# Six plain chunk pairs instead of eight in a fused attention and MLP kernel, with the last v, the exponential, the x additions and three steps of the group schedule moved

## The chip, the core and the metric

The kernel runs on one core of one Trainium2 chip. The metric is the device time of one execution in microseconds: the median of 3 runs before is 1306.22 us (1305.91 to 1307.12). In the text PE is TensorE (matmuls), PEld its weight loads, DVE is VectorE, ACT ScalarE, POOL GpSimd and SP SyncE; an engine executes its instructions in their order. POOL and SP here mostly issue DMAs.

## The reference

Tokens S = 2048, width D = 576, hidden F = 4608. All numbers are float32.

```python
xn = layernorm(x)
return x + A(xn) + B(xn)
# A: q, k, v = heads of xn @ wqkv (32 heads of 18); each token looks at itself and
#    7 earlier tokens, 2 apart; softmax of q.k * 18**-0.5; weighted sum of v; @ wo
# B: h  = gelu(layernorm(xn) @ w1), its four quarters shifted by +1, -1, +2, -2 tokens
#    x1 = xn + h @ w2
#    return x1 + gelu(layernorm(x1) @ w3) @ w4
```

## The kernel before

To keep float32 accuracy on PE, each operand is split into a high part and a low part (a copy on ACT, a subtraction on DVE), and a product is the sum of high x high, high x low and low x high. D = 576 is four and a half times 128, so such a product over D is 14 matmuls of 128 x 512.

The stages follow one another: the norms and q, k, v (written to DRAM as qkvd), the mixing with w1 and w2, then the large MLP (w3, w4) with the attention woven in as background work, and last the product with wo.

**The MLP.** F is cut into 36 chunks of 128, taken in 18 pairs. The first NPL = 8 pairs (line 37) are *plain*: for each pair and each of four blocks of 512 tokens there is a *unit* (loop at line 960) with two `up` (28 matmuls of 512 columns, then gelu) and four `down` of the unit before (48 matmuls of 288 columns). The other NWP = 10 pairs go through *groups* (loop at line 1130): a group treats one pair and 1024 tokens by a Strassen-Winograd scheme in seven products of seven matmuls (49 of 512 columns) and eight downs (96 of 288). There are NQ = 2 x NWP groups; the first NWP take tokens 0 to 1023, the rest tokens 1024 to 2047. In group NWP - 1 and the start of group NWP the seven operands of the second half are read again from DRAM (`get_op`, line 875) and split (`split_op`, line 885). In the code z is the unit's or the group's number counted from the end: z = -1 is the last.

**The order inside a group** is written out by hand: `ORDER` (line 1125) lists products P1 to P7 and downs D0 to D7 as "P1 P2 D0 P6 D1 P5 D2 P7 D3 P4 D4 P3 D5 D6 D7", and `at(item, f)` hangs further work on an item: loads of w3 and w4 (`load_pair`, line 905; `load_w4`, line 554), splits (`split_a`, `split_s`, `split_w4`, line 562), `combine` (line 916), which makes the sums and differences of w3 blocks in place, gelus and their low parts. `keep` (line 1070) copies a product from PSUM on ACT, `z_add` (line 1073) adds a product to it on DVE. A down's result goes either to Y in SBUF (DVE, line 841) or, for the ten token tiles in YD, through a staging tile (ACT, line 836) and an accumulating DMA on POOL's queue to DRAM (line 837). In PSUM two banks alternate for the downs.

w3's raw tile (`w3st`) has one buffer: `load_pair` fills it, `split_a` reads the parts A11, A22 and A12, one of its steps through an accumulating DMA (line 929), `combine` overwrites it, `split_s` reads it with another such DMA, and only then may the next load start.

**The attention** (line 677) is a generator over eight groups of four heads. For each it multiplies q with eight shifted views of k (L735) and sums (L738), adds the mask, takes the maximum and subtracts it, issues the exponential on ACT (L753), and then runs `av` (line 699) for the four heads before: weights times v (L711) summed into po (L715), and a store of po to DRAM (`od`, line 717). q, k, v and po have one buffer each. The load of the next v (line 759) is issued after that store. `bg(us, late)` (line 763) pulls pieces of the generator until a debt of microseconds is used up; each piece yields its assumed cost in us. A piece that yields None holds the generator until a call with `late`: in the plain units every second down, in the groups the item P6. In units 4 and on the rate is 9.4 us for each unit (none in the last two), in the groups 1.6 us for each item less what the group's own DVE work is assumed to cost. At group z = -6, item P4, the attention must be done; its SBUF room then goes to `o_turn` and `load_o` (lines 1108 to 1123), which turn od's tiles (DVE transposes, lines 160 and 161) in groups z = -5 to -2, and `put_o` writes them back for the wo product.

**The other steps that the change touches.** `sums` (line 858) builds the operands T1 to T4 in DRAM in units 5 to 19, by accumulating DMAs on POOL's queue. `load_xa` and `add_x` (lines 845 and 853) add x again: for tiles in YD by an accumulating DMA on POOL's queue, for the six others by a load on SP's queue into one buffer and an addition on DVE one unit later. In the last group w4's last pair is loaded (line 1144) ahead of wo, and split at D2 (line 1228).

Of the kernel before, what the change touches and what calls it, by code (L numbers as in the profile page):

```python
# [10 lines left out]
AF = mybir.ActivationFunctionType  # L11
# [22 lines left out]
YD = (1, 2, 3, 5, 7, 9, 10, 11, 13, 15)  # L34


NPL = 8
NWP = NF // 2 - NPL


# [17 lines left out]
def fused_block(ctx, tc, x, wqkv, wo, w1, w2, w3, w4, out):  # L58
# [618 lines left out]
    def attention(ap):  # L677
        mask = ap.tile([128, TPP, W], F32, name="mask")
        pool.memset(mask, 0.0)
        for w in range(1, W):  # L680
            pool.memset(mask[0:1, 0:DIL * w, W - 1 - w:W - w], -1e9)
        mask4 = mask[:, :, None, :].to_broadcast([128, TPP, GH, W])
        halo = HALO
        qs, ks, vs, Ls, den = {}, {}, {}, {}, {}
        po = ap.tile([128, 2, TPP * GC], F32, name="po")
        o = po[:, 0, :].rearrange("p (x d) -> p x d", d=HD)
        prod = po[:, 1, :].rearrange("p (x d) -> p x d", d=HD)

        def load(name, sel, g, lead, sp=sp):
            t = ap.tile([128, TPP + (halo if lead else 0), GC], F32, name=name)  # L690
            r = sel * NG + g
            sp.dma_start(t[:, (halo if lead else 0):, :],
                         qkvd[r, halo:, :].rearrange("(p j) d -> p j d", p=128))
            if lead:
                sp.dma_start(t[:, :halo, :],
                             qkvd[r, 0:S, :].rearrange("(p j) d -> p j d", p=128)[:, 0:halo, :])
            return t

        def av(g):
            L, v = Ls[g], vs[g]  # L700
            Lf = L.rearrange("p j h w -> p (j h) w")
            dve.tensor_reduce(den[g], Lf, axis=AX.X, op=ALU.add)
            dve.reciprocal(den[g], den[g])
            yield 0.8
            dve.tensor_tensor(Lf, Lf, den[g][:, :, None].to_broadcast([128, TPP * GH, W]),
                              op=ALU.mult)
            yield 0.6
            for w in range(W):
                vv = v[:, DIL * w:DIL * w + TPP, :].rearrange("p j (h d) -> p (j h) d", d=HD)
                dst = prod if w else o  # L710
                dve.tensor_tensor(dst, vv, Lf[:, :, w:w + 1].to_broadcast([128, TPP * GH, HD]),  # L711
                                  op=ALU.mult)
                yield 1.35
                if w:
                    dve.tensor_tensor(o, o, dst, op=ALU.add)  # L715
                    yield 1.35
            sp.dma_start(od.rearrange("(p j) d -> p j d", p=128)[:, :, g * GC:(g + 1) * GC],
                         po[:, 0, :].rearrange("p (j c) -> p j c", c=GC))

        yield None  # L720
        qs[0], ks[0] = load("q", 0, 0, False, pool), load("k", 1, 0, True, pool)
        vs[0] = load("v", 2, 0, True, pool)
        yield None
        for g in range(NG + 1):
            if g < NG:
                q, k = qs[g], ks[g]
                L = Ls[g] = ap.tile([128, TPP, GH, W], F32, name="L", bufs=2)
                Lf = L.rearrange("p j h w -> p (j h) w")
                Lw = Lf.rearrange("p x w -> p w x")
                qf = q.rearrange("p j d -> p (j d)")  # L730
                for w, n in ((0, 1), (1, 1), (2, 2), (4, 2), (6, 2)):
                    dst = po[:, 2 - n:2, :]
                    win = bass.AP(tensor=k.tensor, offset=k.offset + DIL * w * GC,
                                  ap=[list(k.ap[0]), [DIL * GC, n], [1, TPP * GC]])
                    dve.tensor_tensor(dst, qf[:, None, :].to_broadcast([128, n, TPP * GC]), win,  # L735
                                      op=ALU.mult)
                    yield 0.15 + 1.2 * n
                    dve.tensor_reduce(Lw[:, w:w + n, :],  # L738
                                      dst.rearrange("p w (x d) -> p w x d", d=HD),
                                      axis=AX.X, op=ALU.add)  # L740
                    yield 0.15 + 1.2 * n
                if g + 1 < NG:
                    qs[g + 1], ks[g + 1] = load("q", 0, g + 1, False), load("k", 1, g + 1, True)
                mx = den[g] = ap.tile([128, TPP * GH], F32, name="mx", bufs=2)
                dve.tensor_tensor(L, L, mask4, op=ALU.add)
                yield 0.6
                dve.tensor_reduce(mx, Lf, axis=AX.X, op=ALU.max)
                yield 0.6
                dve.tensor_tensor(Lf, Lf, mx[:, :, None].to_broadcast([128, TPP * GH, W]),
                                  op=ALU.subtract)  # L750
                yield 0.6
                yield None
                act.activation(L, L, AF.Exp, scale=float(HD) ** -0.5)  # L753
                if g == 0:
                    yield 4.0
            if g:
                yield from av(g - 1)
                if g < NG:
                    vs[g] = load("v", 2, g, True)

    state = {"gen": None, "debt": 0.0, "hold": False, "done": False}

    def bg(us, late=True):
        if state["gen"] is None or state["done"]:
            return
        state["debt"] = min(state["debt"] + us, 4.0)
        while state["debt"] > 0 and (late or not state["hold"]):
            cost = next(state["gen"], False)
            if cost is False:
                state["done"] = True  # L770
                return
            state["hold"] = cost is None
            state["debt"] -= cost or 0.0


    def temp(t, n=512):
# [183 lines left out]
    for u, (c, b) in enumerate(units):  # L960
# [79 lines left out]
            load_w4(NPL)  # L1040
        if 5 <= u < 21 and u % 2:
            sums((u - 5) // 8, (u - 5) % 8 // 2)
        if 13 <= u < 13 + NT:
            load_xa(u - 13)
        if 14 <= u < 14 + NT:
            add_x(u - 14)
    close_ab()


# [80 lines left out]
    for q in range(NQ):  # L1130
# [6 lines left out]
        if z == -1:  # L1137
            evc_pool.__exit__(None, None, None)
            opc.__exit__(None, None, None)
            EV[0] = (9, 11, 10, 2)  # L1140
            wop = tc.tile_pool(name="wop", bufs=1, reuse_waits="tile")
            wopool = wop.__enter__()
            Wo = wopool.tile([128, 10, D], F32R, name="Wo")
            load_w4(p)
            for k in range(5):
                load_wo(k)
        if q == NWP:
# [64 lines left out]
        elif z < -1:  # L1212
            at("P1", load_w4, p)
            at("D1", split_a, n, (0, 1))
            at("D2", split_a, n, (2,))
            at("P7", combine, n)
            at("D3", split_w4, p, 0)
            at("P4", gelu22)
            at("P4", split_w4, p, 1)
# [5 lines left out]
            if z < -2:  # L1225
                at("D6", load_pair, q + 2 + (q == NWP - 2))
        else:
            at("D2", split_w4, p)
            at("D3", gelu22)
            at("D4", low22)  # L1230
            at("D5", gelu12)
            at("D6", low12)
# [9 lines left out]
        if -4 <= z < -1:  # L1242
            at("P1", put_o, z + 4)
        if z == -2:
            at("D7", put_o, 3)

        if z == -1:
# [134 lines left out]
```

## Time and profile before

| | |
|---|---|
| median of 3 runs | 1306.22 us |
| lowest and highest run | 1305.91 and 1307.12 us |
| the profiled execution | 1301.97 us |
| its span, first to last instruction | 1300.2 us |
| mean granted clock of PE | 0.993 |
| HBM traffic, read and written | 119.73 and 107.28 MB |

Everything but the first three rows of this table is taken from the one profiled execution; the runs beside it carry no profile. "Busy" is the time in which an engine executes; PE's weight loads overlap its matmuls and are counted apart. In rows of waits the engine and the line that waited stand on the left, what it waited for on the right. In rows of time the columns are the start, the length, the engine with its line, the operation, output and inputs, and in brackets the idle time ahead of it with what ended it. SPq and PEq are the engines' sequencers, which issue DMAs and wait.

### The profile page before, as it was taken

Reading aid. Unit: us, or ns where it says so; the run is one execution under the profiler, and the core shown is the slowest. Engines: PE = TensorE matmul, PEld = TensorE weight load, DVE = VectorE, ACT = ScalarE, POOL = GpSimd, SP = SyncE. Lnnn points to the kernel's source line nnn. Section 1 sums busy time; section 2 is a strip of 40 time slices with the busy share of each in tenths; the row PEclk is TensorE's granted clock in tenths of the full one; section 3 lists DMA queues with packets and bytes.
Section 4 is the critical chain, followed back from the end, with each engine's and each line's share of the span. In section 5 each row is a group of like instructions: output and inputs, shape, how many; then the busy total and the mean of one; then the engine's idle time right before and its main releaser. Section 6 shows DMA issues by size and latency. Waiting matters only on the chain.

```text
span 1300.2 us, 19681 instructions
## 1 busy us (share of the span) xinstructions
PE 1266.0 (97%) x7538; PEld 1161.7 (89%) x7538; DVE 944.6 (73%) x1261; ACT 598.2 (46%) x952; POOL 245.2 (19%) x358
## 2 busy tenths in 40 slices
PE   8999999999999999999999999999959999999999
PEld 8999998899888998989899889999848999988898
DVE  6456535778469999999999889999859654665442
ACT  3322226526534434344346656556546555554530
POOL 2011100021221212222221222222112222222100
PEclk9999999999999999999999999999979999999999
DMA  7646874256887878988788777776796658899972
GB/s 210 156 111 143 172 166 144 71 147 177 203 247 152 174 170 202 233 145 223 146 205 185 136 171 159 154 161 112 161 228 106 129 110 180 174 209 195 255 242 83
DMA packets 201374, 219.16 MB, mean 169 GB/s; under 512 B 79152, under 2 KB 137744, under 8 KB 201152
## 3 DMA queue, kind: packets, MB, share of 16 engines
q1 hardware_dynamic: 168912, 151.57, 41.0%
q0 software_dynamic: 32368, 66.34, 31.9%
q8 instruction: 59, 0.97, 0.3%
q14 instruction: 35, 0.29, 0.1%
HBM read 119.73 MB, written 107.28 MB: 175 GB/s over the span
## 4 chain that ended last, share of the span: by engine, by line
PE 78%; DMA 10%; DVE 4%; issue 4%; ACT 2%; SPq 1%; POOL 0%; DVEq 0%; POOLq 0%; ACTq 0%
PE ps L832 27%; PE ps L214 16%; PE cc L1065 13%; PE p L813 13%; PE ps L466 4%; PE ps L313 3%; DMA w3st<-in_B_w_dram 2%; DMA x1n<-xn 1%; DMA yd<-Y 1%; DMA xn<-st 1%; DMA xt<-xn 1%; DMA w3a<-w3st 1%; DMA xt<-xd 1%; DMA wr<-in_A_wo_dram 1%; PE ps L481 1%
## 5 line engine op out<-in xcount | busy, mean ns | idle before, releaser
L832 PEld LDWEIGHTS ps<-w,c 128*128 128x128 f32 x3456 | 474.5, 188 | 27.5 <-DVE Y L841 8.8
L832 PE MATMUL ps<-w,c 128*128 128x288 f32 x3456 | 486.1, 295 | 10.8 <-DVE Y L841 7.0
L837 POOL DMA_DIRECT2D yd<-Y x154 | 137.0, 894 | 464.7 <-ACT Y L836 388.4
L836 ACT COPY Y<-ps 128x576 f32<-128x576 f32 x154 | 97.9, 636 | 151.4 <-PE ps L832 96.5
L807 DVE TENSOR_TENSOR c<-Y,c 128x512 fp32r<-128x512 f32 x144 | 98.4, 685 | 58.8 <-ACT Y L796 42.3
L214 PE MATMUL ps<-WQ,xt 128*128 128x432 f32 x672 | 134.8, 360 | 0.0
L214 PEld LDWEIGHTS ps<-WQ,xt 128*128 128x128 f32 x672 | 125.6, 188 | 5.7
L1065 PE MATMUL cc<-xt,w3s 128*128 128x512 f32 x420 | 108.3, 398 | 13.5 <-DVE Y L1075 13.5
L841 DVE TENSOR_TENSOR Y<-ps,Y 128x576 f32<-128x576 f32 x108 | 81.2, 751 | 49.2 <-PE ps L832 49.0
L1065 PEld LDWEIGHTS cc<-xt,w3s 128*128 128x128 f32 x420 | 76.7, 190 | 27.6 <-DVE Y L1075 14.0
L711 DVE TENSOR_TENSOR po<-v,L 128x1152 f32<-128x1152 f32 x64 | 86.1, 1353 | 14.7 <-DMA v<-qkvd 13.8
L735 DVE TENSOR_TENSOR po<-q,k 128x2304 f32<-128x2304 f32 (+1 forms) x40 | 82.9, 2073 | 13.9 <-issue 11.6
L795 ACT ACTIVATE c<-p 128x512 fp32r<-128x512 f32 x64 | 38.2, 597 | 115.8 <-PE p L813 115.8
L738 DVE TENSOR_REDUCE L<-po 128x128 f32<-128x2304 f32 (+1 forms) x40 | 82.8, 2069 | 0.4
L1071 ACT COPY Y<-cc 128x512 f32<-128x512 f32 x60 | 35.1, 584 | 97.4 <-PE cc L1065 94.1
L121 POOL TENSOR_TENSOR rs<-rs,mhalf 128x1 f32<-128x1 f32 x48 | 30.9, 643 | 258.8 <-DVE rs L120 148.0
L715 DVE TENSOR_TENSOR po<-po 128x1152 f32<-128x1152 f32 x56 | 75.8, 1353 | 0.8
L323 ACT COPY stg<-ps 128x864 f32<-128x864 f32 x24 | 21.2, 881 | 102.8 <-PE ps L214 60.5
L1065 PE MATMUL cc<-x1n,w3a 128*128 128x512 f32 (+1 forms) x280 | 67.9, 393 | 0.0
L1065 PEld LDWEIGHTS cc<-x1n,w3a 128*128 128x128 f32 (+1 forms) x280 | 51.6, 188 | 10.3
L214 PE MATMUL ps<-W,h 128*128 128x288 f32 x384 | 53.5, 295 | 0.0
L813 PE MATMUL p<-xt,w3s 128*128 128x512 f32 x224 | 52.4, 390 | 0.0
(188 smaller groups left out, 1892.6 us busy)
## 6 DMA issues: line engine op xcount, KB each, us to landing
yd<-Y POOLq DMA_DIRECT2D x156, 288.0 KB, 5.2
Y<-in_B_w_dram SPq DMA_DIRECT2D x27, 576.0 KB, 6.7
w3st<-in_B_w_dram SPq DMA_DIRECT2D x52, 256.0 KB, 6.3
qkvd<-stg SPq DMA_DIRECT2D x24, 432.0 KB, 3.5
yd<-ev POOLq DMA_DIRECT2D x26, 288.0 KB, 6.4
xd<-st SPq DMA_DIRECT2D x16, 320.0 KB, 6.0
xd<-big SPq DMA_DIRECT2D x16, 320.0 KB, 7.4
w3st<-in_B_w_dram SPq DMA_DIRECT2D x76, 64.0 KB, 6.5
```

Source lines behind the costliest of these rows:

```text
L214: pe.matmul(ps[:, h, :n], xs(a), ws(b, h), start=i == 0, stop=i == len(PAIRS) - 1)
L711: dve.tensor_tensor(dst, vv, Lf[:, :, w:w + 1].to_broadcast([128, TPP * GH, HD]), op=ALU.mult)
L715: dve.tensor_tensor(o, o, dst, op=ALU.add)
L735: dve.tensor_tensor(dst, qf[:, None, :].to_broadcast([128, n, TPP * GC]), win, op=ALU.mult)
L738: dve.tensor_reduce(Lw[:, w:w + n, :], dst.rearrange("p w (x d) -> p w x d", d=HD), axis=AX.X, op=ALU.add)
L807: dve.tensor_tensor(h[:, 1, :], g, h[:, 0, :].bitcast(F32), op=ALU.subtract)
L813: pe.matmul(ps, W3[f][:, w, :], x1n[b][:, a, :], start=n == 0, stop=n == len(PAIRS) - 1)
L832: pe.matmul(ps[:, k, :HF], h[:, col], w[:, p, k * HF:(k + 1) * HF], start=n == 0, stop=n == len(seq) - 1)
L836: act.copy(e.rearrange("p (h c) -> p h c", h=2), ps[:, :, :HF])
L837: pool.dma_start(yd[t], e, accum_op=ALU.add)
L841: dve.tensor_tensor(yv, ps[:, :, :HF], yv, op=ALU.add)
L1065: pe.matmul(ps, WX[w][:k, v, SLOT[w], :], area[sb][xk][:k, a, :], start=onto is None and i == 0, stop=last and i == len(HALVES) - 1, skip_ ...
```

## The change

The number of plain pairs falls from 8 to 6, so 24 units stand ahead of 24 groups of 12 pairs. The loads and additions of x start with unit 6 instead of 13. In the attention the exponential is put aside (`state["exp"]`) and issued by the next call of `bg` with `late`, by the next exponential, or ahead of the last `av`; the generator does not hold. The last four heads' v is loaded into k's buffer, as soon as the last scores are formed and their maximum is subtracted. `combine` moves from item P7 to D3 in the ordinary groups. The last pair's w4 is loaded at D7 of group z = -2, ahead of `put_o(3)`, instead of at the start of the last group; in the last group `split_w4` goes from D2 to D3 and `gelu22` from D3 to P4.

```diff
-NPL = 8
+NPL = 6
 NWP = NF // 2 - NPL
...
         def av(g):
+            if g == NG - 1:
+                exp_now()
             L, v = Ls[g], vs[g]
...
                 yield 0.6
-                yield None
-                act.activation(L, L, AF.Exp, scale=float(HD) ** -0.5)
+                exp_now()
+                state["exp"] = lambda L=L: act.activation(L, L, AF.Exp, scale=float(HD) ** -0.5)
+                if g == NG - 1:
+                    vs[g] = load("k", 2, g, True)
                 if g == 0:
                     yield 4.0
             if g:
                 yield from av(g - 1)
-                if g < NG:
+                if g < NG - 1:
                     vs[g] = load("v", 2, g, True)
 
-    state = {"gen": None, "debt": 0.0, "hold": False, "done": False}
+    state = {"gen": None, "debt": 0.0, "exp": None, "done": False}
+
+    def exp_now():
+        if state["exp"]:
+            state["exp"]()
+            state["exp"] = None
 
     def bg(us, late=True):
         if state["gen"] is None or state["done"]:
             return
+        if late:
+            exp_now()
         state["debt"] = min(state["debt"] + us, 4.0)
-        while state["debt"] > 0 and (late or not state["hold"]):
+        while state["debt"] > 0:
             cost = next(state["gen"], False)
             if cost is False:
                 state["done"] = True
                 return
-            state["hold"] = cost is None
-            state["debt"] -= cost or 0.0
+            state["debt"] -= cost
...
-        if 13 <= u < 13 + NT:
-            load_xa(u - 13)
-        if 14 <= u < 14 + NT:
-            add_x(u - 14)
+        if 6 <= u < 6 + NT:
+            load_xa(u - 6)
+        if 7 <= u < 7 + NT:
+            add_x(u - 7)
...
             Wo = wopool.tile([128, 10, D], F32R, name="Wo")
-            load_w4(p)
...
-            at("P7", combine, n)
+            at("D3", combine, n)
             at("D3", split_w4, p, 0)
...
         else:
-            at("D2", split_w4, p)
-            at("D3", gelu22)
+            at("D3", split_w4, p)
+            at("P4", gelu22)
...
         if z == -2:
+            at("D7", load_w4, NPL + pair(q + 1))
             at("D7", put_o, 3)
```

## The prediction

> **What bounds the kernel now.** I read the page first, then the busy time by stretches, then PE's waits, then the order of time around each place where PE stood.
>
> ```profile
> PE 1266.0 (97%) x7538; PEld 1161.7 (89%) x7538; DVE 944.6 (73%) x1261; ACT 598.2 (46%) x952; POOL 245.2 (19%) x358
> ```
>
> PE is the bound as a whole: it is busy 1266.0 of 1300.2 us, so time goes away only with matmuls or with one of PE's few gaps.
>
> ```profile
> 500.00:709.00 209.00, 208.57 (x1243) 189.89 (x1243) 199.96 (x187) 87.47 (x138) 49.54 (x57) 1.00 0.86 183
> ...
> 766.00:927.00 161.00, 161.00 (x967) 146.30 (x966) 152.90 (x168) 94.14 (x145) 38.22 (x45) 1.00 0.72 148
> 927.00:977.00 50.00, 35.17 (x209) 31.49 (x208) 31.70 (x36) 25.29 (x39) 7.76 (x9) 0.86 0.89 208
> 977.00:1138.00 161.00, 161.00 (x961) 146.18 (x961) 101.78 (x140) 91.90 (x146) 38.26 (x45) 1.00 0.70 140
> ```
>
> The columns are stretch, length, then busy us of PE, PEld, DVE, ACT, POOL, the granted clock, DMA share and GB/s. Plain units (500 to 709) and groups with attention on DVE (766 to 927) leave PE without a gap although DVE is 95% busy; groups without attention (977 to 1138, from 1011 on) bring DVE down to 63%. The exception is 927 to 977 with the clock at 0.86, where the first half of the tokens gives way to the second.
>
> ```profile
> DVE po L711 <- DMA v<-qkvd: 13.8, 1, 13.8
> PE cc L1065 <- DVE Y L1075: 13.5, 1, 13.5
> ```
>
> Totals, times, longest. DVE stood once for the last heads' v; PE stood behind it, because the z_add that frees a PSUM bank (L1075) was queued behind the waiting L711.
>
> **The change, part by part.**
>
> *Two plain chunks become four groups.* Starts of successive ups (28 matmuls) and of successive P1 (14):
>
> ```profile
> 502.35 6.38 PE p L813 x28
> ...
> 693.25 6.39 PE p L813 x28
> ...
> 788.00 3.23 PE cc L1065 x14
> ...
> 908.57 3.23 PE cc L1065 x14
> ```
>
> Fifteen units take 693.25 - 502.35 = 190.90 us, 12.73 each. Five groups with attention take 120.57 us, 24.11 each. A group does the work of two units, so it saves 2 x 12.73 - 24.11 = 1.35, and four save 5.4 us. The price is attention: eighteen units (4 to 21) carry it instead of twenty-six, and in the built order it now ends early in group 18 instead of group 11.
>
> ```profile
> L711 DVE TENSOR_TENSOR po<-v,L 128x1152 f32<-128x1152 f32 x64 | 86.1, 1353 | 14.7 <-DMA v<-qkvd 13.8
> ...
> L735 DVE TENSOR_TENSOR po<-q,k 128x2304 f32<-128x2304 f32 (+1 forms) x40 | 82.9, 2073 | 13.9 <-issue 11.6 <-DMA od<-po 1.8
> ```
>
> The groups that it fills hold eight or nine operations of 1.35 us, or five or six of 2.07, some 11 us each, as groups 1 to 8 held before. So DVE stays at the 95% that the stretch 766 to 927 stood. Value 5.4; ends 2 (each newly filled group loses a few tenths) and 6.4.
>
> *The last v goes into k's buffer.* SP's queue around the wait:
>
> ```profile
> 941.51 1.74 SPq L883 DMA_DIRECT2D x1n<-xn  x3
> 945.87 0.53 SPq L717 DMA_DIRECT2D od<-po  x1
> 946.45 2.22 SPq L692 DMA_DIRECT2D v<-qkvd  x1
> ```
>
> v has one buffer, so its load is issued only when the previous heads are finished, behind their store of po; for the earlier heads the next scores come between, for the last nothing. In the changed order the last v is loaded right after the last scores, before the previous heads' weighted sum (fifteen operations of 1.35 us), so that wait goes. What is late next?
>
> ```profile
> 945.83 1.06 ACT L892 ACTIVATE x1n<-x1n 128x1024 fp32r<-128x1024 f32 x1 [4.51 <-DMA x1n<-xn]
> ...
> 947.59 0.63 ACT L894 ACTIVATE x1n<-x1n 64x512 fp32r<-64x512 f32 x1
> 962.37 0.64 ACT L836 COPY Y<-ps 128x576 f32<-128x576 f32 x1 [14.15 <-PE ps L832]
> ```
> ```profile
> 957.45 3.29 PE L1065 MATMUL cc<-xt,w3s 128*128 128x512 f32 x7 [13.54 <-DVE Y L1075]
> ...
> 977.09 3.39 PE L1065 MATMUL cc<-x1n,w3a 128*128 128x512 f32 x14
> ```
>
> Without the wait P3 starts at 957.45 - 13.54 = 943.9 and, at some 1.6 us each, it and the down after it end near 947.1, before ACT is through with its first operand (947.59 + 0.63 = 948.2). Of ACT's 50.00 - 25.29 = 24.7 idle us in 927 to 977 these two waits are 18.7: behind them its split_ops stand nearly unbroken, so ACT bounds the rest of the stretch, and all of it moves up by ACT's 14.15 us. One thing may not follow: the second operand's load was issued until 941.51 + 1.74 = 943.25.
>
> ```profile
> 936.26 9.55 DMA x1n<-xn
> ```
>
> Landing like the first one (9.55 us after its first issue; the second's began near 940.4) it is there at 949.9, and ACT wants it at 948.8: 1.1 lost. Value 14.15 - 1.1 = 13.0; ends 6 (the first rival) and 15.
>
> *The x additions.* They move from units 13 to 29 to units 6 to 22.
>
> ```profile
> L855 DVE TENSOR_TENSOR Y<-Y,rz 128x576 f32<-128x576 f32 x6 | 4.5, 750 | 0.0
> ```
>
> Six of 0.75 us on DVE, ten accumulating DMAs on POOL's queue and six loads on SP's, none more than before. In 500 to 709 they lay beside units that ran without a gap; in units 6 to 13 they meet the T sums on the same POOL queue. If the cover were gone, they cost 4.5. Value 0.5; ends 0 and 4.5.
>
> *The exponential put aside* changes no instruction; the generator goes on instead of holding until P6. Four exponentials fall into groups instead of two.
>
> ```profile
> L753 ACT ACT_TABLE_LOAD x8 | 10.3, 1283 | 0.1
> ...
> 795.08 1.28 ACT L753 ACT_TABLE_LOAD   x1
> ```
>
> Each brings two table loads of 1.28 us. The one at 795.08 lies in the five groups above, which cost 24.11: hidden, 0; if ACT were late, two more groups lose up to 2 x 1.28 + 0.63 = 3.2 each.
> The Trainium skill, "ScalarE: Activation LUTs", section "What ACT_TABLE_LOAD costs", adds 1380 ns of drain to each load, which speaks against this part: an estimate from it, four more switches unhidden, is 5.5 us more, 1287. No wait of PE in this trace shows such a cost.
>
> *combine goes from P7 to D3.* In most groups the order on DVE stays as it was. In the four groups that turn the attention's result, P7's o_turn now comes ahead of combine:
>
> ```profile
> 1132.53 0.68 DVE L807 TENSOR_TENSOR c<-Y,c 128x512 fp32r<-128x512 f32 x1
> 1135.61 2.34 DVE L921 TENSOR_TENSOR w3st<-w3st 128x384 f32<-128x384 f32 x4 [2.40 <-issue]
> 1137.87 0.70 DVE L160 STREAM_TRANSPOSE big<-Y 128x512 f32<-128x512 f32 x1
> 1138.50 0.27 DVE L161 STREAM_TRANSPOSE big<-Y 128x128 f32<-128x128 f32 x1
> ```
> ```profile
> 1140.73 3.44 PE L832 MATMUL ps<-w,c 128*128 128x288 f32 x24 [1.45 <-DVE Y L841]
> ...
> 1166.02 3.44 PE L832 MATMUL ps<-w,c 128*128 128x288 f32 x24 [0.95 <-DVE Y L841]
> ...
> 1191.81 3.44 PE L832 MATMUL ps<-w,c 128*128 128x288 f32 x24 [1.47 <-DVE Y L841]
> ```
>
> DVE stands 2.40 us ahead of combine and then turns for 0.9 (1137.87 to 1138.77) while PE waits for the down's addition behind it. The turn fits into the idle time, and the addition comes 0.9 earlier: 3 x 0.9 = 2.7. Ends 0 (the turn's input late) and 3.9 (all three waits).
>
> *The last w4 is loaded one group earlier*, ahead of put_o, and split at D3.
>
> ```profile
> 1202.21 1.94 SPq L559 DMA_DIRECT2D Y<-in_B_w_dram  x1
> ```
> ```profile
> 1210.73 1.15 ACT L566 CAST w<-Y 128x1152 fp32r<-128x1152 f32 x1 [5.58 <-DMA Y<-in_B_w_dram]
> ```
> ```profile
> 1212.42 2.79 PE L1065 MATMUL cc<-xt,w3a 128*128 128x512 f32 x7 [2.72 <-ACT Y L1071]
> 1215.01 2.43 PE L832 MATMUL ps<-w,c 128*128 128x288 f32 x12
> 1217.28 1.78 PE L1065 MATMUL cc<-xt,w3s 128*128 128x512 f32 x7
> ```
> ```profile
> 1214.00:1216.00 2.00, 2.00 (x8) 1.71 (x8) 0.47 (x1) 1.17 (x2) 0.16 (x1) 0.50 1.05 249
> ```
>
> The load is issued at 1202.21, ACT waits 5.58 for it, and the copy that PE's P4 needs stands behind. Its raw place is free once the previous split is done, just ahead of the addition that PE awaits at 1191.81, so the load starts some 10 us earlier; the wait goes. PE gains 2.72 and the slow clock after it: 7 matmuls in 2.79 instead of 1.78 and 12 in 2.43 instead of the 1.75 of a usual down, 1.7 more. Value 4.4; ends 2 (the reads of wo and o late next) and 5.
> The Trainium skill, "TensorE: Matmul & The Clock Gate", section "What's actually happening", lets the clock fall only after an idle window of about 3.4 us; by that this gap would cost 2.72 alone and the sum be 1283.2. The trace differs: clock 0.50 after a 2.72 us gap.
>
> **The sum.** 5.4 + 13.0 - 0.5 + 2.7 + 4.4 = 25.0 us. Against the profiled execution's 1301.97 us (span 1300.2) that gives 1277.0. The runs' median is 1306.22, 4.25 longer than the profiled one; I take the gain from the median: 1281.2.
>
> **The rivals.**
> 1. *The middle is bound by the operands' loads.*
>
> ```profile
> 940.00:945.00 5.00, 3.92 (x23) 3.14 (x21) 0.36 (x1) 0.59 (x1) 0.00 (x0) 1.00 1.06 318
> ```
>
> The DMA engines are full there. If each of the five later operands comes 1.4 us after ACT wants it, 7 of the 13.0 are lost: 1288. Against it: the store and the v load leave this place in the queue.
> 2. *The x additions cost their full 4.5* in the fuller units: 1285.2.
> 3. *DVE waits at the same place for something else*, for instance the store of po that the next scores overwrite, now issued after all operand loads. It would have to last as long as v did; the 13.0 are lost: 1294. Against it: two scores that use the other half, and the splits, lie between.
> 4. *Slower: filled groups miss the w3 loop.* Load, split, combine and the next load form a ring; where it didn't close in time, P1 came 25.78 us apart:
>
> ```profile
> 1118.40:1144.18 25.78, 24.33 (x146) 21.97 (x146) 14.65 (x25) 13.37 (x21) 5.62 (x8) 1.00 0.95 213
> ```
>
> If attention delays combine so in all eighteen groups that carry it, 18 x 1.67 = 30 us eat the gain: 1311. It decides where DVE demand passes a group's 24.1 us, at some 12 us of attention in every group; for it speaks DVE's 95%, against it the 24.11 of five such groups.
>
> **How the numbers follow.** Forecast 0.76 (its own span 1275 to 1286), first rival 0.11, second 0.05, third 0.04, slower 0.04. The range 1275 to 1290 takes in the first three, and leaves out the last two and a little of the forecast's edges. 0.2% is 2.6 us, about what a measurement tells from no change: faster 0.95, within 0.01, slower 0.04.
>
> **What would show it.** Right: no wait of DVE for v; PE's wait of 13.5 gone and the clock at 1.00 through the middle; P1 near 24.1 apart in groups with attention after the middle too; waits for L841 in the late groups under 0.6; no wait of ACT for w4. Wrong: a new wait of DVE for a DMA, ACT waiting for operand loads at each split, units 6 to 13 over 12.73, or groups near 25.7.

## The result, and the profile after

The changed kernel takes 1296.15 us (median of 6 runs, 1294.97 to 1301.92) beside 1305.39 for the kernel before: a ratio of 0.9936, 95% interval 0.9917 to 0.9956. It is faster, by 9.2 us where 25.0 were forecast, and outside the range of 1275 to 1290. The profiled execution took 1294.97 us with a span of 1293.2, 7.0 less than before.

Busy time of the engines, from the page after; then stretches of its time with the columns of the prediction's table (groups 1 to 10, the middle, groups 12 to 17, groups 18 and 19, the three late groups):

```profile
PE 1263.3 (98%) x7510; PEld 1159.4 (90%) x7510; DVE 966.4 (75%) x1295; ACT 617.2 (48%) x978; POOL 252.5 (20%) x366
```
```profile
634.65:887.12 252.47, 243.88 (x1452) 220.67 (x1451) 226.41 (x251) 144.85 (x222) 59.63 (x70) 0.99 0.70 150
887.12:920.50 33.38, 29.36 (x171) 26.64 (x170) 27.48 (x30) 21.32 (x33) 6.06 (x7) 0.95 1.04 257
920.50:1065.60 145.10, 141.92 (x848) 128.41 (x847) 133.16 (x152) 85.90 (x134) 34.31 (x41) 1.00 0.65 133
1065.60:1113.72 48.12, 48.12 (x292) 43.88 (x291) 31.57 (x45) 26.53 (x42) 11.95 (x15) 1.00 0.80 170
1113.72:1191.31 77.59, 74.50 (x438) 67.43 (x437) 45.10 (x75) 40.24 (x63) 17.70 (x21) 0.98 0.92 214
```

The middle went from 44.62 to 33.38 us, near the forecast. But the groups that carry attention, which had lost 3.34 us in all before, now have more gaps: PE is busy 243.88 of 252.47 us in the first row. DVE is less busy there (90%) than the 95% of before, which speaks against a want of DVE's time. What waits, in the groups (totals, times, longest):

```profile
DVE w3st L931 <- issue: 13.2, 5, 4.5
...
DVE po L713 <- DMA od<-po: 4.7, 1, 4.7
...
DVE po L737 <- DMA od<-po: 4.1, 1, 4.1
```
```profile
PE ps L842 <- DVE Y L851: 19.2, 15, 3.5
```

DVE stands ahead of `combine` (L931) and for po's store, and PE behind it for a down's addition (L851). At L931 the profile names nothing that was waited for ("issue"); what ends there is read from the landing times below. Starts of successive P1 give the account. A group without a stall takes 24.06 us; what is over that in groups 1 to 10 is 5.75 (group 1), 3.38 (4), 1.73 (5), 0.87 (9) and 0.14 (10), together 11.87, against 3.34 in groups 1 to 8 of before; in the groups behind the middle it is 3.95 (3.32 of it in group 16), against 0.

| part | us gained |
|---|---|
| eight units (102.15) less four groups of 24.06 | +5.9 |
| stalls in filled groups, first half: 11.87 instead of 3.34 | -8.5 |
| stalls in filled groups, second half | -4.0 |
| the middle, 44.62 to 33.38 | +11.2 |
| the three late groups, 76.85 to 77.59 | -0.7 |
| the last group, 42.55 to 39.18 | +3.4 |
| ahead of the units and behind the groups | -0.3 |
| sum, as the spans show | +7.0 |

**The first kind of stall.** Group 1 on SP, POOL, DVE and PE, and from the DMA issues the time from issue to landing:

```profile
644.33 0.35 SPq L692 DMA_DIRECT2D q<-qkvd  x1
644.73 0.44 SPq L692 DMA_DIRECT2D k<-qkvd  x1
645.21 0.47 SPq L695 DMA_DIRECT2D k<-qkvd  x1
```
```profile
646.60 0.78 POOL L939 DMA_DIRECT2D w3a<-w3st  x1 [0.44 <-ACT w3a L938]
```
```profile
k<-qkvd SPq DMA_DIRECT2D x1, 504.0 KB, 10.1
...
w3a<-w3st POOLq DMA_DIRECT2D x1, 48.0 KB, 8.9
```
```profile
655.57 2.34 DVE L931 TENSOR_TENSOR w3st<-w3st 128x384 f32<-128x384 f32 x4 [4.53 <-issue]
```
```profile
659.89 4.73 PE L842 MATMUL ps<-w,c 128*128 128x288 f32 x24 [2.78 <-DVE Y L851]
```

Attention's loads of q and k, 1656 KB on SP's queue, are issued from 644.33 to 645.21; the last lands at 645.21 + 10.1 = 655.3. The 48 KB that `split_a` adds into w3a go out at 646.60 on POOL's queue and land at 646.60 + 8.9 = 655.5; combine, which overwrites their source, starts at 655.57. In group 2, with no such loads ahead, the same transfer lands 3.4 us after its issue and DVE does not wait. Groups 5 and 9 show the same (7.6 and 5.8 to landing). Not all of group 1's 5.75 is this: at its start PE also waits 0.86 us for the split of w4 (L569), with or without the transfer.

**The second kind.** Group 16: the store of the heads before the last, and DVE:

```profile
1022.12 0.53 SPq L719 DMA_DIRECT2D od<-po  x1
```
```profile
1023.31 0.69 DVE L707 TENSOR_TENSOR L<-L,mx 128x512 f32<-128x512 f32 x1
```
```profile
1028.67 2.63 DVE L713 TENSOR_TENSOR po<-k,L 128x1152 f32<-128x1152 f32 x2 [4.67 <-DMA od<-po]
```

The last heads' v is there (it is read from k's buffer), but the first product is written into po, which the store of 1022.12 still reads. In group 4 the scores that use both halves of po wait 4.14 us for such a store.

**A late group**, the one behind 1113.72:

```profile
1124.25 6.19 SPq L168 DMA_DIRECT2D xd<-big  x4
```
```profile
1125.14 0.77 POOL L939 DMA_DIRECT2D w3a<-w3st  x1 [1.27 <-ACT w3a L938]
```
```profile
1129.25 0.27 DVE L161 STREAM_TRANSPOSE big<-Y 128x128 f32<-128x128 f32 x1
1132.27 2.33 DVE L931 TENSOR_TENSOR w3st<-w3st 128x384 f32<-128x384 f32 x4 [2.76 <-DMA xd<-big]
```

The turn does come ahead of combine now, and combine waits 2.76 us all the same: put_o's stores go out just before the w3a transfer.

### The profile page after: what moved, and what is told of

Same layout as the page of the kernel before. It is cut to its first block, busy times and chain, and to the rows that moved or that the text cites. A ratio compares the mean times of both kernels' runs of the same rounds, so it can differ in the third digit from the quotient of the medians.

```text
span 1293.2 us, 19747 instructions
## 1 busy us (share of the span) xinstructions
PE 1263.3 (98%) x7510; PEld 1159.4 (90%) x7510; DVE 966.4 (75%) x1295; ACT 617.2 (48%) x978; POOL 252.5 (20%) x366
## 4 chain that ended last, share of the span: by engine, by line
PE 64%; issue 12%; DMA 10%; DVE 8%; POOL 3%; ACT 2%; SPq 2%; POOLq 0%; DVEq 0%; ACTq 0%
PE ps L842 21%; PE ps L214 16%; PE cc L1075 11%; PE p L823 8%; PE ps L466 4%; DMA w3a<-w3st 3%; PE ps L313 3%; POOL yd L847 2%; DMA x1n<-xn 2%; DVE w3st L931 2%; DVE w L569 1%; DMA w3st<-in_B_w_dram 1%; DVE Y L851 1%; PE ps L481 1%; DVE po L737 1%
## 5 line engine op out<-in xcount | busy, mean ns | idle before, releaser
L842 PE MATMUL ps<-w,c 128*128 128x288 f32 x3456 | 493.1, 297 | 23.8 <-DVE Y L851 19.2
L1075 PE MATMUL cc<-xt,w3s 128*128 128x512 f32 (+1 forms) x504 | 128.2, 394 | 0.0
L1075 PEld LDWEIGHTS cc<-xt,w3s 128*128 128x128 f32 (+1 forms) x504 | 91.0, 188 | 16.1
L851 DVE TENSOR_TENSOR Y<-ps,Y 128x576 f32<-128x576 f32 x108 | 81.1, 751 | 32.4 <-PE ps L842 31.8
L1081 ACT COPY Y<-cc 128x512 f32<-128x512 f32 x72 | 42.1, 585 | 121.7 <-PE cc L1075 118.4
L1075 PE MATMUL cc<-x1n,w3a 128*128 128x512 f32 (+1 forms) x336 | 81.4, 393 | 0.0
L713 DVE TENSOR_TENSOR po<-v,L 128x1152 f32<-128x1152 f32 x56 | 75.7, 1353 | 0.9
L1075 PEld LDWEIGHTS cc<-x1n,w3a 128*128 128x128 f32 (+1 forms) x336 | 61.9, 188 | 12.4
L805 ACT ACTIVATE c<-p 128x512 fp32r<-128x512 f32 x48 | 28.7, 598 | 83.6 <-PE p L823 83.6
L931 DVE TENSOR_TENSOR w3st<-w3st 128x384 f32<-128x384 f32 x92 | 51.2, 556 | 22.3 <-issue 13.2
L1085 DVE TENSOR_TENSOR Y<-cc,Y 128x512 f32<-128x512 f32 x72 | 49.3, 684 | 8.5 <-ACT Y L1081 6.4
```

Source lines behind the costliest of these rows:

```text
L842: pe.matmul(ps[:, k, :HF], h[:, col], w[:, p, k * HF:(k + 1) * HF], start=n == 0, stop=n == len(seq) - 1)
L851: dve.tensor_tensor(yv, ps[:, :, :HF], yv, op=ALU.add)
L931: dve.tensor_tensor(st[:, :, o, :], st[:, :, o, :], st[:, :, i, :], op=op)
L1075: pe.matmul(ps, WX[w][:k, v, SLOT[w], :], area[sb][xk][:k, a, :], start=onto is None and i == 0, stop=last and i == len(HALVES) - 1, skip_ ...
```

## The experiments

The theory tested here: the gain was lost to transfers that meet at fixed places in a group, a small one in the chain of w3 behind attention's large ones, and po's store (the *collision theory*). Rivals: DVE has no room in filled groups (*overload*), or another edit makes them late. Each kernel has its own runs of the kernel before beside it (medians 1305.8 to 1308.3), so ratios are compared, in brackets with their 95% intervals. The lengths of groups and waits are from one profiled execution of each kernel.

**The four groups alone, and the rest alone.** `npl8_rest` is the changed kernel with `NPL = 8`; `npl6_only` the kernel before with

```diff
-NPL = 8
+NPL = 6
-        if 13 <= u < 13 + NT:
+        if 6 <= u < 6 + NT:
```

and the same for `add_x`.

> The changed kernel with eight plain chunks again; every other edit stays. Collision theory (the time lost is in groups where attention's bulk loads are issued just ahead of the 48 KB accumulating DMA on w3a, or where DVE waits for po's store; moving eight units of attention into groups put more of them there): with fewer filled groups most of these stalls go, the other edits give what the profile after shows of them (middle 11.2, last group 3.4, late groups -0.7), so 1305.4 - 13.9 = about 1291.5, below the changed kernel. Overload theory (DVE has no room in any filled group): the same sign, 1290 to 1293, so this run does not part the two. Theory that another edit (exponential put aside, combine at D3) makes the filled groups late: groups of 25.7 to 29 here too, 1299 or more.

> The kernel before with six plain chunks and the x additions from unit 6 on (they must fit into 24 units); nothing else of the change. Collision and overload theories: the four more groups bring 5.6 and lose 8 to 12 in stalls, and the wait for the last v stays, so 1305.4 + 2 to 6 = 1307 to 1312. Theory of another edit: the filled groups run at 24.1 to 24.3 and the time is 1305.4 - 5.6 = 1299.8.

Measured: 1301.04 (0.9949, 0.9927 to 0.9971) and 1325.2 (1.0127, 1.0084 to 1.0170). Both expectations are missed. With eight chunks the rest of the change brings 0.5%, with six 1.9%; the four groups cost 1.3% alone, and with the rest (0.9936 against 0.9949) no difference can be told. So the edits are not terms of a sum. The 1301 of npl8_rest is where the rival "another edit" put it, but npl6_only speaks against that rival: it has none of the other edits, and its filled groups ahead of the middle lose 13.4 us (11.87 in the changed kernel; group 1 takes 31.34 there, its w3a transfer landing 7.8 us after its issue). In the profile of npl8_rest the time from the first P1 to the wo product did fall, from 518.64 to 511.74; the plain stretch, longer by as much (392.00 instead of 385.10), hid it. In the middle of npl8_rest DVE stands where it stood for v before:

```profile
954.95 1.36 DVE L713 TENSOR_TENSOR po<-k,L 128x1152 f32<-128x1152 f32 x1 [7.77 <-DMA od<-po]
```

**The w3a transfer taken away.** `pool_add`, and `before_add` for the kernel before:

```diff
-            pool.dma_start(dst[32:64, 0].bitcast(F32), src[32:64, 0], accum_op=ALU.add)
+            pool.tensor_tensor(dst[32:64, 0], dst[32:64, 0].bitcast(F32), src[32:64, 0], op=ALU.add)
```

> The changed kernel with the accumulating DMA of each w3a and w3s (48 or 64 KB, SBUF to SBUF) replaced by an addition of the same 32 partitions on GpSimd: no transfer stands in the chain from split to combine any more. Collision theory: stalls of the first kind go in filled groups and in the late groups (27.68 falls to 25 or less), 9 to 12 us come back: 1284 to 1287; waits for po's store stay. Overload theory: 1294 to 1298. A third way: GpSimd's addition is slow or takes DVE's time (24 pairs of additions), 1297 or more.

> The kernel before with one thing changed: the 32-partition addition on GpSimd in place of the accumulating DMA. Collision theory: the three late groups (25.78, 25.28, 25.79, sum 76.85) fall to 24.1 each, 4.7, and the collided w3a transfers of two filled groups give 1 to 2.5 more; the wait for the last v stays: 1305.5 - 6 = 1298.5 to 1301. If the transfer of w3a only matters with more attention in the groups: 1304 to 1306, and the late groups keep their 76.9.

Measured: 1292.62 (0.9892, 0.9856 to 0.9929) and 1301.77 (0.9962, 0.9943 to 0.9981). The three late groups of pool_add:

```profile
1117.30:1189.47 72.17, 72.17 (x437) 65.81 (x436) 47.74 (x76) 40.07 (x63) 19.76 (x22) 1.00 0.97 221
```

PE has no gap: 24.06 each instead of 25.86; in before_add they take 72.18. In both kernels the late groups' stalls were this transfer; before_add's time is a little above its 1298.5 to 1301. The waits ahead of combine are gone in the filled groups too. Two kinds of stall remain in pool_add, the waits for po's store:

```profile
DVE po L737 <- DMA od<-po: 5.1, 1, 5.1
...
DVE po L713 <- DMA od<-po: 2.7, 1, 2.7
```

and, at the start of group 1, a longer wait for the split of w4, with PE's clock down behind it (7 matmuls in 3.13 us instead of 1.78):

```profile
646.54 1.83 PE L842 MATMUL ps<-w,c 128*128 128x288 f32 x10 [1.47 <-DVE w L569]
648.17 3.13 PE L1075 MATMUL cc<-xt,w3s 128*128 128x512 f32 x7
```

So group 1 still takes 28.43 us instead of 29.80. Groups 5 and 9 fall to 24.06, but group 4 takes 28.99, and the ten filled groups ahead of the middle lose 11.5 us in all, as before the remedy: most of what the run gained behind the first P1 (7.3 us) lies in the late groups (5.4). It missed 1284 to 1287 for this and because its plain stretch, from the first up of unit 2 (they count from 0) to the first P1, took 288.5 us and not 283.0. That is taken up below. Its interval overlaps the changed kernel's (0.9917 to 0.9956) a little.

**The loads moved away from it.** `defer` keeps the transfer and moves attention's loads:

```diff
+            if state["aside"]:
+                state["loads"].append((g, sel, lambda: fill(t, sel, g, lead, sp)))
...
             for f in plan.get(it, ()):
                 f()
+            if it == "D6" and z < -6 and q != NWP - 1:
+                loads_now()
```

> The changed kernel with attention's loads of q, k and v put aside inside groups and issued right behind the w3st load at D6 (where SP has to wait for the w3s DMA anyway), so that they are over before the next group's accumulating DMA on w3a. Collision theory: the w3a DMA lands within 6 us of its issue in every filled group, the groups at 29.81, 25.79, 24.93 and 24.70 fall to 24.1 to 24.4, about 8 to 9 us come back: 1287 to 1289; the two waits for po's store (27.4 each) may stay. Overload theory: the DVE work is the same, the groups stay above 25 in sum, 1294 to 1298.

Measured: 1292.66 (0.9890, 0.9858 to 0.9922), beside 1287 to 1289 expected. From first P1 to the wo product it took 606.75 us instead of 613.49, 6.7 less with all of DVE's work; the plain stretch was 288.2, which hides most of it, and the intervals overlap a little. Group 1 falls from 29.80 to 25.48 and groups 5 and 9 to 24.06 with the transfer still in place; in group 1 it lands 3.1 us after its issue instead of 8.9, while DVE runs the same operations behind that issue in the same order. So it is the loads that delay it, and not DVE's work. But the moved loads meet the next group's transfer instead: in group 6 it lands 6.7 us after its issue, where at most 6 was expected, and the group takes 25.68. Overload would have left the 613.

**po's waits taken away.**

```diff
-                for w, n in ((0, 1), (1, 1), (2, 2), (4, 2), (6, 2)):
+                for w, n in ((0, 1), (1, 1), (2, 1), (3, 1), (4, 2), (6, 2)):
...
+            if g == NG - 1:
+                store = ap.tile([128, TPP, GC], F32, name="q").rearrange("p j c -> p (j c)")
```

> The changed kernel with nothing of the w3a transfer touched, but two edits for the buffer po: scores take windows 2 and 3 one at a time (so that the half of po that the store reads is written 5.4 us of DVE work later, for 0.3 us more work per heads), and the last heads' sum goes into q's buffer, which is free by then. Collision theory: no DVE wait for po's store is left (4.67 and 4.14 in the profile after), the two groups of 27.4 fall to 24.1 to 25, the ones at 29.81, 25.79 and 27.68 stay: 1296.15 - 5 = 1290 to 1292. Overload theory: the 2.4 us of added DVE work make it 1296 to 1299.

> Both remedies together: the two po edits and the 32-partition addition on GpSimd in place of the accumulating DMA. Collision theory: the remedies add up, since they take away different waits: the addition alone gave 1292.62, the po waits of its profile (5.1 and 2.7, in groups of 28.99 and 26.17) are worth 5 to 7 more: 1285.5 to 1287.5. Overload theory: no better than the addition alone, 1292 to 1295.

Measured: po_free 1291.63 (0.9882, 0.9857 to 0.9908), add_po 1289.61 (0.9874, 0.9846 to 0.9902). po_free's time came as expected, but not for the expected reason alone: the groups at 29.80 and 25.79, which were to stay, took 25.50 and 24.05, and groups 6 and 8 lost 1.9 and 1.2 instead, since attention's loads go out at other times. DVE does not wait for the store any more and group 16 takes 24.19, but group 4 still takes 28.30: there combine now waits 2.78 us for the w3a transfer, which the wait for po had hidden. add_po missed by 2 to 4 us and cannot be told from either remedy alone; its plain stretch was 289.8, groups 1 and 4 still took 28.45 and 26.00, and six more lost 0.5 to 1.2 us each.

**Four edits undone one at a time**, each by the lines of the diff above.

> The changed kernel with the last heads' v in its own buffer again, loaded when the heads before are finished. If the edit is worth what the prediction counts, DVE waits for v once more, now in one of the groups behind the middle, and PE behind it: 13 to 14 us, 1296 + 13 = 1309. If the shorter middle came from attention's other phase alone (the wait would have been hidden or fallen elsewhere), 1296 to 1300, and the middle keeps its 33.4.

> The changed kernel with the exponential as before: the generator holds until a late point instead of putting the ACTIVATE aside. The prediction's own value for this edit is 0, and the collision theory keeps it within 3 us of 1296 (the holding moves attention's phase, so other groups can be hit). If putting aside is what made the filled groups late, 1286 to 1290. If holding is what costs (attention then ends later, nearer to the late groups), 1300 to 1310, which would also explain why six plain chunks alone gave 1325.

> The changed kernel with combine at P7 again in all groups of the common form. The prediction counted 2.7 for its move to D3 in the three late groups, whose sum is 77.59 now and was 76.85. If the move is worth something but a later w3a transfer ate it: combine at P7 is asked for one eviction earlier, each collided transfer holds D3's addition as well, and the time is 1298 to 1303. If the move is worth nothing: 1296. If the move itself made the late groups late: 1293 to 1295, and 77.59 falls to 76.9 or less.

> The changed kernel with the last w4 loaded in the last group again, its split at D2 and gelu22 at D3. The last group with what follows took 39.34 instead of 42.71: if that is the w4 load, 1296 + 3.4 = 1299.5, an ACT wait for the transfer and a PE wait for ACT or DVE are back in the last group, and the clock falls there. If the shorter last group comes from something else (DVE free of combine earlier), 1296 to 1297.

`v_undone`: 1304.18 (0.9977, 0.9954 to 1.0000), between its two expectations. The wait for v is back, in group 16, which takes 33.34 instead of 27.38:

```profile
DVE po L713 <- DMA v<-qkvd: 9.3, 1, 9.3
```

The middle keeps 33.20. So the edit is worth some 6 us in that group, and the shorter middle comes from elsewhere: with six chunks attention's end, where the wait is, lies five groups behind the middle. npl6_only, which has none of the other edits, confirms it: its middle takes 33.85.

`exp_undone`: 1312.49 (1.0052, 1.0031 to 1.0074), a little beyond the 1300 to 1310 of its last case, and the dearest edit to undo. The last operation of attention in exp_undone and in the changed kernel:

```profile
1102.34 1.35 DVE L717 TENSOR_TENSOR po<-po 128x1152 f32<-128x1152 f32 x1
```
```profile
1072.17 1.35 DVE L717 TENSOR_TENSOR po<-po 128x1152 f32<-128x1152 f32 x1
```

Held at each exponential, attention ends 19.7 us into group 18 instead of 6.6, pressed out where it must be done; groups 17, 19 and the last late one then take 30.28, 28.90 and 27.85. This is probably also most of why six chunks alone gave 1325: its groups 19 to 22 are long too (26.32 to 29.20).

`comb_undone`: 1301.26 (0.9957, 0.9939 to 0.9975). The time is that of its first case, in which the move is worth something, but the intervals overlap, its plain stretch was 291.9, and the three late groups take 78.13; in the profiles that have combine at D3 and the transfer (after, defer, v_undone, w4_undone) they take 75.97 to 78.67. So the move shows no worth of its own.

`w4_undone`: 1300.90 (0.9974, 0.9946 to 1.0001), near its 1299.5. ACT and PE wait in the last group again, which takes 43.98 instead of 39.18:

```profile
1208.14 1.15 ACT L566 CAST w<-Y 128x1152 fp32r<-128x1152 f32 x1 [5.85 <-DMA Y<-in_B_w_dram]
```
```profile
1209.83 3.35 PE L1075 MATMUL cc<-xt,w3a 128*128 128x512 f32 x7 [2.98 <-ACT Y L1081]
1212.98 3.04 PE L842 MATMUL ps<-w,c 128*128 128x288 f32 x12
```

**The plain stretch.** In v_undone, comb_undone, w4_undone and defer the plain units are the same program as in the changed kernel, and took 287.05, 291.85, 285.58 and 288.22 us where its own profile has 282.95: that profile is the best case (its run is the fastest of the six). Most of the difference lies in one unit, which begins at 590 to 594 and takes 17.06, 18.08, 14.08 and 18.06 us in these four, 13.65 in the changed kernel's profile and 12.73 as a rule. In defer:

```profile
605.65 2.92 PE L856 MATMUL ps<-w,c 128*128 128x288 f32 x12 [4.05 <-ACT Y L860]
```
```profile
596.80 1.06 ACT L916 ACTIVATE x1n<-x1n 128x1024 fp32r<-128x1024 f32 x1 [2.00 <-DMA x1n<-xn]
```

Near 600 the first operands are split; their loads are queued behind a store of po, a load of v and a load of x, ACT waits for them ahead of an eviction, and PE for that. add_oq_defer (below), which puts attention's loads aside there and leaves the additions of x where they are, has 12.73 for this unit: what makes it long is attention's load of v. No six-chunk kernel shows DVE waiting for a row of x. `x_from_13` is npl8_rest with `load_xa` and `add_x` from units 13 and 14 again.

> npl8_rest (1301.0) with the x additions from unit 13 on, as in the kernel before; they differ in this alone. If the earlier additions cost nothing, as the profile after alone suggests, the same 1300 to 1302 and a plain stretch of 392 in both. If the 7 us by which the plain stretch of npl8_rest was longer than before's (392.0 against 384.9) come from loading and adding x earlier, 1294 to 1296 and 385 to 386.

Measured: 1294.40 (0.9907, 0.9871 to 0.9943) against 0.9949 for npl8_rest. The point estimates are 5.5 us apart; the intervals overlap a little. The time is as expected for a cost of the x additions; the plain stretch is not, 388.2 against 392.0, less apart than executions of one program are. But in npl8_rest the loss can be followed. DVE stood for a row of x, whose load is queued behind one of v; the exponential on ACT then waited for DVE, the eviction behind it too, and PE for that:

```profile
DVE Y L865 <- DMA rz<-in_A_x_dram: 7.3, 1, 7.3
```
```profile
618.56 0.63 ACT L755 ACTIVATE L<-L 128x512 f32<-128x512 f32 x1 [4.63 <-DVE L L751]
```
```profile
619.77 3.25 PE L842 MATMUL ps<-w,c 128*128 128x288 f32 x12 [4.12 <-ACT Y L846]
```

The unit in which this falls and the next took 18.47 and 13.45 us, 6.5 over two usual ones. x_from_13 has no such wait.

**All remedies.** `add_oq_defer` joins pool_add, the last sum in q's buffer, and defer, with the loads put aside in the last four plain units too; `add_oq_defer_8` has eight chunks; `add_oq_defer_sing` the scores' windows 2 and 3 one at a time, as in po_free.

> A candidate for a better kernel: the changed one with the addition on GpSimd, the last heads' sum in q's buffer, and attention's loads put aside in the groups (issued at D6) and in the last four plain units (issued behind the last operand load of the first half). Collision theory: the w3a waits, one po wait and the crowd of loads at the end of the plain chunks go, the time is 1281 to 1286, and the stretch from the second up to the first product is back from 288 to 283. Overload theory: 1288 to 1292, with the stalls spread over other groups.

> The candidate add_oq_defer with eight plain chunks instead of six, nothing else. If a group with attention costs 24.1 and only collided transfers made it more, the four groups are worth 5.6 against the eight units here: 1285.1 + 5.6 = 1290.7 (1289 to 1292). If the filled groups are dearer by themselves (DVE full), the two kernels are within 1.5 us of each other, or this one is the faster.

> The candidate add_oq_defer with the scores' windows 2 and 3 taken one at a time, so that the wait for po's store in the fifth group (4.55, a group of 28.5 with the slow clock behind it) finds 5.4 us of other work. Collision theory: 1285.1 - 3 to - 4 = 1281 to 1282. If DVE's room is what counts, its 2.4 us of added work eat it: 1284.5 to 1287.

Measured: 1285.07 (0.9831, 0.9802 to 0.9861), 1296.03 (0.9906, 0.9874 to 0.9938) and **1282.46** (0.9808, 0.9779 to 0.9838). The first came as expected, the second missed its 1289 to 1292, the third came 0.5 us over its 1281 to 1282. The third beats both kernels: its interval lies wholly under the changed kernel's 0.9917 to 0.9956. Its ten groups that carry attention ahead of the middle:

```profile
636.83:882.63 245.80, 243.46 (x1453) 220.69 (x1451) 237.67 (x254) 145.13 (x222) 73.17 (x71) 0.99 0.67 150
```

DVE is 97% busy, more than in the changed kernel, and PE's gaps are 2.3 us instead of 8.6: overload falls. The stalls of the filled groups are 5.2 us ahead of the middle and 1.5 behind it, instead of 11.87 and 3.95, and the three late groups take 72.18. Nine of these ten groups average 24.2 us; group 1 keeps 27.8, by the wait for the split of w4 that pool_add showed. The plain stretch is back at 281.7 in add_oq_defer. With these remedies the two chunks are worth 0.75% (0.9906 against 0.9831, intervals apart), 9.8 us, more than the 5.4 of the prediction. But in the profiles the eight units took 113.6 us, 11.8 over 8 x 12.73, against 99.9 for the four groups: in the eight-chunk kernel DVE waits 7.0 for a row of x, and two units lose 6.6 us behind it. So most of the 9.8 is that stall and not the groups' merit. The third differs from the first by the wait in group 4, which is gone (28.49 to 24.06); in the time the difference is not clear, as the intervals overlap.

## Why the prediction was wrong

The sign was right; the time was missed by 15 us because three steps looked at engines where transfers decided. By the profiles the six terms, forecast and measured, are: groups 5.4 and -6.6 (5.9 - 8.5 - 4.0), middle 13.0 and 11.2, x additions -0.5 and none seen, exponential 0 and not to be parted in them, combine 2.7 and -0.7 (the late groups), w4 4.4 and 3.4.

1. *Two chunks become four groups, 5.4: failed.* The step was "So DVE stays at the 95% that the stretch 766 to 927 stood". DVE did not even reach it (90%). The step took five groups of before as a sample of any filled group, but in those PE lost almost nothing to the w3a transfer. It priced neither that transfer nor po's store; filled groups cost 12.5 us more than before, and with all remedies 9.1 of their 15.8 us of stalls were gone. The trace of before had the case, just ahead of the sample: in group 1 (26.89 us) the w3a transfer, behind a store of po and a load of v, landed 6.1 us after its issue, and combine waited:

```profile
755.94 2.34 DVE L921 TENSOR_TENSOR w3st<-w3st 128x384 f32<-128x384 f32 x4 [2.90 <-issue]
```

The fourth rival had the ring (load, split, combine, next load) and called for DVE demand as what decides; the ring was right, the trigger was a transfer, in five groups (1, 4, 5, 9 and 16; in 4 and 16 po's store, outside the ring) and not eighteen.
2. *The last v, 13.0: size near, cause wrong.* The middle gained 11.2, but v_undone keeps its 33.2 and npl6_only has 33.85 without this edit: the wait had moved away with attention's end. The prediction itself has attention end "early in group 18 instead of group 11", and still counts the wait in the middle as this edit's gain; that the sum came near there is luck. The step "so that wait goes. What is late next?" then asked ACT alone. Next late was po's store (4.67 in group 16; 7.77 at the old place with eight chunks), the third rival, which was given 0.04. The edit is worth about 6, in group 16.
3. *The x additions, 0.5: as a term not refuted, but another is missing.* No six-chunk kernel shows a wait for a row of x. What the sum leaves out is attention's load of v ahead of the operands' loads at the end of the plain units: 13.65 to 18.08 us in that unit instead of 12.73. Beside the profile after it would have looked right (282.95 against 385.10 - 8 x 12.73 = 283.3); four further executions show 2 to 9 more. With eight chunks the earlier additions did cost 6.5 us in one profile, more than the second rival's 4.5.
4. *The exponential, 0: failed as a term.* Its table loads are hidden, as said: groups 2 and 6 contain one exponential each and take 24.06. But putting it aside is what lets attention end in time with six chunks; undoing it costs 1.16% (1.0052 against 0.9936), 15 us. The prediction priced instructions and not the holding that it removed. The drain of the Trainium skill, "ScalarE: Activation LUTs", section "What ACT_TABLE_LOAD costs", does not show in those two groups.
5. *combine, 2.7: failed.* "The turn fits into the idle time" was so, but the idle time belonged to the w3a transfer behind put_o's stores: it lands 6.7 to 7.0 us after its issue in the late groups now and took 5.7 to 6.0 before. What the three groups could gain is shown by before_add: 4.7 us, with the transfer gone and combine where it was.
6. *The last w4, 4.4: right.* 3.4 in the profiles of before and after, 4.8 in that of w4_undone, and 0.4% between the ratios, whose intervals overlap a little. (The other sum that the prediction gives there, without the slow clock, comes to 1282.9 from its own numbers and not 1283.2; nothing hangs on it.)

The best kernel runs at 1282.5, beside a forecast of 1281.2. That is a coincidence: it has remedies that the forecast did not count, and its gain is not made of the forecast's terms. Some 6.7 us of stalls in its filled groups remain, not all of them explained.

## What to carry to other kernels

When work is moved beside a stage that runs without gaps, list the stage's small transfers that an engine waits for, and what bulk transfers will be issued in the few microseconds ahead of each: free engine time says nothing of them. A wait that ends last hides the next one at the same instruction; look at every buffer that the instruction touches, its output too. Where a background task has a place by which it must be done, price an edit by what it does to that end.

## What the runs showed of the hardware

A 48 KB transfer on POOL's queue landed 3.4 us after its issue with nothing large ahead, and 8.9, 7.6, 5.8 and 7.0 with 1216 to 1656 KB just issued on SP's queue, in groups 1 and 5 within 0.2 us of the last large load's landing. The Trainium skill, "DMA: Bandwidth & Descriptors", section "Queues, rings and completion order", says that a transfer's semaphore increment lands only after every earlier write of the same DMA engine, across its queues. Group 1 agrees, 655.5 beside 655.3. The runs do not part this rule from a plain sharing of the engines: in group 9 the transfer landed at 855.2, ahead of the last load issued before it (855.7).

The clock fell after some short gaps: behind 2.78 us 24 matmuls took 4.73 us (row above), and in the late group behind 1.83 us

```profile
1136.60 4.96 PE L842 MATMUL ps<-w,c 128*128 128x288 f32 x24 [1.83 <-DVE Y L851]
```

where behind 2.34 us, in v_undone, they took the usual time:

```profile
664.13 3.44 PE L840 MATMUL ps<-w,c 128*128 128x288 f32 x24 [2.34 <-DVE Y L849]
```

The 1.83 us cost 1.83 + 4.96 - 3.44 = 3.35. The Trainium skill, "TensorE: Matmul & The Clock Gate", section "What's actually happening", asks for an idle window of about 3.4 us; here 1.83 sufficed in one place and 2.34 did not in another, so the length of a gap alone does not decide, and what does is not shown.

GpSimd's addition of 32 x 512 took 1.28 to 3.32 us in pool_add, and a subtraction of 0.68 us on DVE took 1.76 beside one, just ahead of the split of w4 that group 1 waits for:

```profile
643.05 1.61 POOL L939 TENSOR_TENSOR w3s<-w3s,w3st 32x512 fp32r<-32x512 f32 x1 [6.04 <-ACT w3s L938]
```
```profile
643.46 1.76 DVE L817 TENSOR_TENSOR c<-Y,c 128x512 fp32r<-128x512 f32 x1
```

The same program's plain stretch varied by 9 us between executions, most of it in the one unit named above, so one profile could not settle the third term; a difference of under some 5 us between single profiles is read as an edit's effect only where a wait for the thing that the edit moves comes or goes with it.
